# Linformer attention and an MLP mixer: the first batch's front part in head pairs with TensorE transposes, its up-projections all ahead, and another order of loads

## The chip, the cores and the metric

The kernel runs on one core of a Trainium2 chip. The metric is the device time of one execution in microseconds (us); smaller is better. Before the change the median of three runs is 519.97 us (519.9 to 520.43).

## The reference

Eight batches, 8 heads, 1024 positions, 64 dimensions a head, all inputs float32:

```python
k_proj = np.einsum('ks,bhsd->bhkd', E, k)        # 64 x 64 per head
v_proj = np.einsum('ks,bhsd->bhkd', F, v)
scores = (1.0 / np.sqrt(64)) * np.matmul(q, k_proj.transpose(0, 1, 3, 2))
attn = softmax(scores)                            # over 64 columns
x = np.matmul(attn, v_proj)                       # then heads side by side: batch x 1024 x 512
xt = x.transpose(0, 2, 1)
h = np.maximum(xt @ w_tok1, 0.0) @ w_tok2         # 1024 -> 256 -> 1024, over positions
u = x + h.transpose(0, 2, 1)
h2 = np.maximum(u @ w_ch1, 0.0) @ w_ch2           # 512 -> 1536 -> 512, over channels
out = u + h2
```

## The kernel before

Everything on the chip is bfloat16, with float32 sums in PSUM. The work of a batch has two parts.

The **front part** (`front_units`) makes `u`. `kv_proj` contracts k and v with E and F over the positions (`kv_ps`), `k_transpose` turns the projected keys (`kt_ps`, `kT`), `scores` multiplies them with the transposed queries `qT` for two heads at a time and takes the exponential (`s_ps`, `a_sb`), `attend` multiplies with the projected values for one head and divides by the sum (`o_ps` of line 195, `rdn`, `x_sb`). Then come the token mixing, `token1` (2 pieces, `h_ps`, `hT_sb`) and `token2` (8 pieces, `u_ps`, `u_sb`): each piece of `token1` needs x of all heads. Two transposes are done by DMA, issued by SyncE (SP): q into `qT`, in two halves of four heads (line 133), and `u_sb` into `uT`, in two halves of 512 positions (line 229).

The **back part** (`back_blocks`) mixes the channels in two halves of 512 positions: 12 blocks of `ch1` (4 matmuls each, the up-projection, `g_ps`, then a ReLU on ScalarE into `gT`), then 12 blocks of `ch2` (4 matmuls each, the down-projection, `o_ps` of line 265; every third one ends a row block, which VectorE adds to `u_sb` and SP sends out). That is 192 matmuls of 512 columns in a batch.

Batch 0's front part is written first, alone. After it the back part of batch b is written with the front units of batch b + 1 strewn between its blocks (lines 299 to 304). The queue of each engine is in order, but a scheduler sets that order from the written one, so the order that counts is that of the built program. All loads go through GpSimd's DMA queue (POOL) and turn float32 into bfloat16: E, F, then batch 0 (four pieces of two heads each for k, v and q), the token weights, `wc1_sb` in four pieces, `wc2_sb` in four pieces, batch 1 (two pieces each for k, v and q), batch 2 and so on. `k_sb`, `v_sb`, `q_sb` and `qT` have two buffers each. PSUM pools: `psC` three buffers (`g_ps`, `o_ps` of line 265), `psA` two (`s_ps`, `o_ps` of line 195), `psS` one (`kv_ps`, `kt_ps`, `h_ps`, `u_ps`). `out_pool` has four buffers for `o_sb`.

Of the kernel before, what the change touches and what calls it, by code (L numbers as in the profile page):

```python
# [15 lines left out]
def kernel(  # L16
# [13 lines left out]
    nc = tc.nc  # L30
# [37 lines left out]
    def load(b, parts):  # L68
        tiles = []
        for name, src in (("k_sb", k), ("v_sb", v), ("q_sb", q)):  # L70
            tiles.append(kv_pool.tile([P, H, NSI, D], BF16, tag=name, name=name))
# [32 lines left out]
    loaded[1] = load(1, 2)  # L104
# [23 lines left out]
    def front_units(b):  # L128
# [18 lines left out]
        def kv_proj():  # L147
# [86 lines left out]
        units = [kv_proj, k_transpose]  # L234
# [11 lines left out]
    def back_blocks(b):  # L246
# [4 lines left out]
        def ch1(i, cc):  # L251
# [83 lines left out]
```

## Time and profile before

| what | value |
|---|---|
| median of 3 runs | 519.97 us |
| the profiled execution's own time | 519.9 us |
| its span, first to last instruction | 517.9 us |
| outside the span | 2.0 us |
| TensorE (PE) busy | 449.0 us, 87% |
| VectorE (DVE) and ScalarE (ACT) busy | 163.0 us and 163.2 us, 31% and 32% |
| first matmul of the back part (`g_ps`) | 88.09 us after the span's start |

In the rows below, PE is TensorE's matmuls, SP is SyncE and POOL is GpSimd; "SPq" is SP's queue, which issues DMAs. `[12.41 <-DMA qT<-q_sb]` at a row's end says that the engine was idle for 12.41 us just before and that the landing of that DMA ended the wait. `x8` is the number of instructions merged in the row. Line numbers are those of the kernel before.

### The profile page before, as it was taken

How to read it: one execution, taken by the hardware profiler on the slowest of the kernel's cores; microseconds unless marked ns; L12 is line 12 of the kernel's file. 1: busy time of each engine (PE TensorE's matmuls, PEld its weight loads, DVE VectorE, ACT ScalarE, POOL GpSimd, SP SyncE). 2: the span in 40 equal slices, each digit the busy share in tenths (PEclk: the TensorE clock that was granted, in tenths of full speed). 3: DMA queues.
4: the chain of work that ended last, by engine and by line, in shares of the span. 5: the costliest groups of instructions: out<-in, count | busy, mean ns of one | idle time of the engine just before them, and what ended most of it. 6: DMA issues, size and time to landing. Idle time of an engine off the chain costs nothing.

```text
span 517.9 us, 5765 instructions
## 1 busy us (share of the span) xinstructions
PE 449.0 (87%) x2384; PEld 209.1 (40%) x2384; DVE 163.0 (31%) x300; ACT 163.2 (32%) x265; POOL 49.0 (9%) x72
## 2 busy tenths in 40 slices
PE   1300751999999999999999999999999999999997
PEld 0100320445444444454444443544444444544443
DVE  2100530044523332253335141624242423432102
ACT  0101100544144322623162507150534144332250
POOL 7422201121020101110020002000000000000000
PEclk9999975999999999999999999999999999999999
DMA  8999999999759823993597057903111230123112
GB/s 125 207 188 197 206 197 200 186 201 182 160 117 200 171 61 104 188 181 55 146 149 177 1 143 125 199 22 102 61 42 41 78 86 27 55 62 101 42 41 81
DMA packets 105530, 63.54 MB, mean 123 GB/s; under 512 B 68641, under 2 KB 96801, under 8 KB 105505
## 3 DMA queue, kind: packets, MB, share of 16 engines
q0 software_dynamic: 29728, 29.63, 35.5%
q1 hardware_dynamic: 75776, 33.56, 25.9%
q8 instruction: 18, 0.29, 0.2%
q14 instruction: 8, 0.06, 0.0%
HBM read 59.24 MB, written 16.78 MB: 147 GB/s over the span
## 4 chain that ended last, share of the span: by engine, by line
PE 78%; DMA 12%; SPq 4%; ACT 3%; DVE 1%; POOL 1%; issue 1%; POOLq 0%; ACTq 0%
PE o_ps L265 32%; PE g_ps L254 29%; DMA q_sb<-in_q_dram 6%; PE u_ps L222 5%; PE h_ps L213 5%; DMA wc_sb<-in_moe_w_ch_dram 4%; SPq L133 4%; PE kv_ps L151 2%; PE o_ps L195 2%; PE s_ps L183 2%; DMA k_sb<-in_k_dram 1%; ACT gT L258 1%; DMA uT_172<-u_sb 1%; DVE kp_sb L156 1%; ACT kp_sb L157 1%; PE kt_ps L168 1%
## 5 line engine op out<-in xcount | busy, mean ns | idle before, releaser
L258 ACT ACTIVATE gT<-g_ps 128x512 bf16<-128x512 f32 x192 | 113.1, 600 | 224.8 <-PE g_ps L254 224.5
L265 PE MATMUL o_ps<-wc_sb,gT 128*128 128x512 bf16 x768 | 182.3, 379 | 0.0
L254 PEld LDWEIGHTS <-wc_sb 128*128 128x128 bf16 x768 | 72.7, 98 | 99.0 <-issue 19.9
L265 PEld LDWEIGHTS <-gT 128*128 128x128 bf16 x768 | 72.6, 98 | 80.1 <-issue 2.6
L226 DVE TENSOR_TENSOR u_sb<-u_ps,x_sb 128x512 bf16<-128x512 f32 x64 | 44.2, 690 | 118.0 <-PE u_ps L222 118.0
L272 DVE TENSOR_TENSOR o_sb<-o_ps,u_sb 128x512 f32<-128x512 f32 x64 | 44.2, 691 | 78.1 <-PE o_ps L265 78.1
L188 ACT ACTIVATE a_sb<-s_ps 128x1024 bf16<-128x1024 f32 x32 | 32.0, 1031 | 50.8 <-PE s_ps L183 50.6
L203 DVE TENSOR_TENSOR x_sb<-o_ps,rdn 128x512 bf16<-128x512 f32 x64 | 44.2, 691 | 2.2
L222 PE MATMUL u_ps<-hT_sb,wt_sb 128*128 128x512 bf16 x128 | 39.9, 394 | 5.4 <-DVE u_sb L226 4.7
L202 DVE RECIPROCAL rdn<-o_ps 128x8 f32<-128x8 f32 x64 | 13.1, 204 | 74.3 <-PE o_ps L195 74.3
L213 PE MATMUL h_ps<-x_sb,wt_sb 128*128 128x512 bf16 x128 | 32.0, 395 | 1.7 <-DVE x_sb L203 1.1
L183 PE MATMUL s_ps<-qT,kT 64*64 64x512 bf16 x128 | 12.5, 423 | 24.3 <-DMA qT<-q_sb 24.1
L75 POOL DMA_DIRECT2D k_sb<-in_k_dram x18 | 13.5, 750 | 150.4 <-PE kv_ps L152 137.9
L195 PEld LDWEIGHTS <-a_sb 128*128 128x128 bf16 x256 | 20.2, 102 | 17.7 <-DVE x_sb L203 3.1
L222 PEld LDWEIGHTS <-wt_sb 128*128 128x128 bf16 x128 | 18.5, 145 | 21.2 <-issue 11.1
L151 PE MATMUL kv_ps<-k_sb,ET_sb 128*64 128x512 bf16 x64 | 17.2, 413 | 9.8 <-DMA k_sb<-in_k_dram 9.8
L156 DVE CAST kp_sb<-kv_ps 64x512 bf16<-64x512 f32 x8 | 5.5, 683 | 55.8 <-PE kv_ps L152 55.8
L80 POOL DMA_DIRECT2D q_sb<-in_q_dram x18 | 13.2, 739 | 101.7 <-DMA qT<-q_sb 91.9
L254 PE MATMUL g_ps<-uT_172,wc_sb 128*128 128x512 bf16 x48 | 12.1, 413 | 11.0 <-DMA uT_172<-u_sb 11.0
L213 PEld LDWEIGHTS <-wt_sb 128*128 128x128 bf16 x128 | 13.0, 101 | 18.4 <-issue 4.6
L217 ACT ACTIVATE hT_sb<-h_ps 128x512 bf16<-128x512 f32 x16 | 9.6, 597 | 27.5 <-PE h_ps L213 27.5
L152 PE MATMUL kv_ps<-v_sb,FT_sb 128*64 128x512 bf16 x64 | 17.0, 413 | 0.7 <-DMA v_sb<-in_v_dram 0.7
(54 smaller groups left out, 272.7 us busy)
## 6 DMA issues: line engine op xcount, KB each, us to landing
out_dram<-o_sb SPq DMA_DIRECT2D x64, 256.0 KB, 2.1
k_sb<-in_k_dram POOLq DMA_DIRECT2D x14, 512.0 KB, 9.7
v_sb<-in_v_dram POOLq DMA_DIRECT2D x14, 512.0 KB, 11.5
q_sb<-in_q_dram POOLq DMA_DIRECT2D x14, 512.0 KB, 8.7
wc_sb<-in_moe_w_ch_dram POOLq DMA_DIRECT2D x8, 384.0 KB, 19.3
k_sb<-in_k_dram POOLq DMA_DIRECT2D x4, 256.0 KB, 8.1
v_sb<-in_v_dram POOLq DMA_DIRECT2D x4, 256.0 KB, 8.6
q_sb<-in_q_dram POOLq DMA_DIRECT2D x4, 256.0 KB, 10.0
```

Source lines behind the costliest of these rows:

```text
L151: nc.tensor.matmul(kv_ps[0:KP], ET_sb[:, si, :], k_sb[:, :, si, :], start=a, stop=z)
L183: nc.tensor.matmul(s_ps[dst * KP : (dst + 1) * KP, h % 2, :], kT[rows, h, :], qT[rows, h].rearrange("p j s -> p (j s)"), start=True, stop= ...
L188: nc.scalar.activation(out=a_sb, in_=s_ps, func=ACT.Exp, scale=scale)
L195: nc.tensor.matmul(o_ps[:, j // 2, (j % 2) * 2 * D1 : (j % 2 + 1) * 2 * D1], a_sb[:, h % 2, j * P : (j + 1) * P], vb[:, h // 2, h % 2].rea ...
L203: nc.vector.tensor_tensor(out=x_sb[:, :, h * D : (h + 1) * D].rearrange("p (n c) d -> p n c d", n=2), in0=o4[:, :, :, 0:D], in1=rdn[:, :, ...
L213: nc.tensor.matmul(h_ps, wt1_sb[:, si, t * P : (t + 1) * P], x_sb[:, si, :], start=(si == 0), stop=(si == NSI - 1),)
L222: nc.tensor.matmul(u_ps, wt2_sb[:, t, si::NSI], hT_sb[:, t, :], start=(t == 0), stop=(t == TC - 1),)
L226: nc.vector.tensor_add(out=u_sb[:, si, :], in0=u_ps, in1=x_sb[:, si, :])
L254: nc.tensor.matmul(g_ps, wc1_sb[:, dc, cc * P : (cc + 1) * P], uT[i][:, :, dc, :], start=(dc == 0), stop=(dc == DMC - 1),)
L258: nc.scalar.activation(out=st["gT"][:, cc, :], in_=g_ps, func=ACT.Relu)
L265: nc.tensor.matmul(o2_ps, st["gT"][:, cc, ss * P : (ss + 1) * P], wc2_sb[:, cc, :], start=(cc == 0), stop=(cc == CC - 1),)
L272: nc.vector.tensor_add(out=o_sb, in0=o2_ps, in1=u_sb[:, si, :])
```

## The change

- The load function is split in two; batch 0's loads stay in their order, and batch 1's loads now stand ahead of `wc2_sb`.
- Batch 0's front part is written out by hand. `kv_proj` runs in four parts of two heads, each over columns of 128. q is transposed by TensorE (`q_transpose_pe`, eight 128x128 transposes for a head pair into `t_ps`, one copy by VectorE). The token mixing goes by head pair with 128 columns (`token1_pair`, `token2_pair`), and `u_sb` is transposed by TensorE (`u_transpose_pe`, four transposes and a copy by ScalarE). Only positions 0 to 511 of `u` are made before the back part begins, and one of the four pieces of the other half; the other three pieces and the transposes of the second half are put between the first five blocks of the back part.
- Batch 0's back part runs both up-projections first (24 blocks), then both down-projections. The front units of batch 1 start after block 16 and are spread over blocks 17 to 44.
- For the later batches, the DMA transposes of q are written with the first units of the front part and no longer ahead of all blocks.

```diff
--- before.py
+++ after.py
...
-    loaded = {0: load(0, 4)}
+
+    load_kv(0, HP)
+    load_q(0, HP)
...
+    load_kv(1, 2)
+    load_q(1, 2)
     wc2_sb = const.tile([P, CC, DM], BF16, name="wc2_sb")
     for c in range(0, CC, CC // 4):
         nc.gpsimd.dma_start(
             out=wc2_sb[:, c : c + CC // 4],
             in_=moe_w_ch2.rearrange("(cc p) d -> p cc d", p=P)[:, c : c + CC // 4],
         )
-    loaded[1] = load(1, 2)
...
-        for h in range(0, H, H // 2):
-            nc.sync.dma_start_transpose(
-                out=qT[:, h : h + H // 2].rearrange("p h j s -> p (h j) s"),
-                in_=q_sb[:, h : h + H // 2].rearrange("p h si d -> p (h si d)"),
-            )
...
+        def q_transpose_pe(hp):
+            t_ps = psC.tile([P, 2, NJ, P], BF16, tag="c", name="t_ps")
+            for h in range(2):
+                for j in range(NJ):
+                    nc.tensor.transpose(
+                        t_ps[:, h, j, :],
+                        q_sb[:, 2 * hp + h, 2 * j : 2 * j + 2, :].rearrange("p s d -> p (s d)"),
+                        ident,
+                    )
+            nc.vector.tensor_copy(out=qT[:, 2 * hp : 2 * hp + 2], in_=t_ps)
+
+        def kv_proj(parts=1):
             kv_ps = psS.tile([P, H, D], F32, tag="s", name="kv_ps")
-            for si in range(NSI):
-                a, z = si == 0, si == NSI - 1
-                nc.tensor.matmul(kv_ps[0:KP], ET_sb[:, si, :], k_sb[:, :, si, :], start=a, stop=z)
-                nc.tensor.matmul(
-                    kv_ps[KP : 2 * KP], FT_sb[:, si, :], v_sb[:, :, si, :], start=a, stop=z
-                )
+            hn = H // parts
+            for h in range(0, H, hn):
+                hs = slice(h, h + hn)
+                for si in range(NSI):
+                    a, z = si == 0, si == NSI - 1
+                    nc.tensor.matmul(
+                        kv_ps[0:KP, hs], ET_sb[:, si, :], k_sb[:, hs, si, :], start=a, stop=z
+                    )
+                    nc.tensor.matmul(
+                        kv_ps[KP : 2 * KP, hs], FT_sb[:, si, :], v_sb[:, hs, si, :],
+                        start=a, stop=z,
...
+        def token1_pair(hp):
+            cols = slice(hp * P, (hp + 1) * P)
+            h_ps = psC.tile([P, TC, P], F32, tag="c", name="hp_ps")
+            for t in range(TC):
+                for si in range(NSI):
+                    nc.tensor.matmul(
+                        h_ps[:, t, :], wt1_sb[:, si, t * P : (t + 1) * P], x_sb[:, si, cols],
+                        start=(si == 0), stop=(si == NSI - 1),
+                    )
+            nc.scalar.activation(out=hT_sb[:, :, cols], in_=h_ps, func=ACT.Relu)
+
+        def token2_pair(hp, i):
+            cols = slice(hp * P, (hp + 1) * P)
+            u_ps = psC.tile([P, NJ, P], F32, tag="c", name="up_ps")
+            for ss in range(NJ):
+                for t in range(TC):
+                    nc.tensor.matmul(
+                        u_ps[:, ss, :], wt2_sb[:, t, i * NJ + ss :: NSI], hT_sb[:, t, cols],
+                        start=(t == 0), stop=(t == TC - 1),
+                    )
+            rows = slice(i * NJ, (i + 1) * NJ)
+            nc.vector.tensor_add(out=u_sb[:, rows, cols], in0=u_ps, in1=x_sb[:, rows, cols])
+
+        def u_transpose_pe(hp, i):
+            t_ps = psA.tile([P, NJ, P], BF16, tag="a", name="ut_ps")
+            for ss in range(NJ):
+                nc.tensor.transpose(
+                    t_ps[:, ss, :], u_sb[:, i * NJ + ss, hp * P : (hp + 1) * P], ident
+                )
+            nc.scalar.copy(out=uT[i][:, :, hp, :], in_=t_ps)
+
+        if b == 0:
+            kv_proj(HP)
+            k_transpose()
+            q_transpose_pe(0)
+            q_transpose_pe(1)
+            scores(0)
+            q_transpose_pe(2)
+            scores(1)
+            attend(0)
+            attend(1)
+            q_transpose_pe(3)
+            scores(2)
+            attend(2)
+            attend(3)
+            scores(3)
+            attend(4)
+            attend(5)
+            token1_pair(0)
+            attend(6)
+            attend(7)
+            token1_pair(1)
+            token1_pair(2)
+            token2_pair(0, 0)
+            token2_pair(1, 0)
+            token1_pair(3)
+            token2_pair(2, 0)
+            u_transpose_pe(0, 0)
+            u_transpose_pe(1, 0)
+            token2_pair(3, 0)
+            u_transpose_pe(2, 0)
+            token2_pair(0, 1)
+            u_transpose_pe(3, 0)
+            return [
+                lambda: token2_pair(1, 1),
+                lambda: (u_transpose_pe(0, 1), token2_pair(2, 1)),
+                lambda: (u_transpose_pe(1, 1), token2_pair(3, 1)),
+                lambda: u_transpose_pe(2, 1),
+                lambda: u_transpose_pe(3, 1),
+            ]
+
+        units = [kv_proj, lambda: (k_transpose(), q_transpose())]
+        if b > 1:
+            units = [lambda: (q_transpose(), kv_proj()), k_transpose]
...
-            st["gT"] = gT_pool.tile([P, CC, S2], BF16, tag="gT", name="gT")
-
-        blocks = []
+            st["gT", i] = gT_pool.tile([P, CC, S2], BF16, tag="gT", name="gT")
+
+        up, down = [], []
         for i in range(2):
-            for cc in range(CC):
-                if cc == 0:
-                    blocks.append(lambda i=i: (half(i), ch1(i, 0)))
-                else:
-                    blocks.append(lambda i=i, cc=cc: ch1(i, cc))
-            for ss in range(NJ):
-                blocks += [lambda i=i, ss=ss, p=p: ch2(i, ss, p) for p in range(CC // 4)]
-        return blocks
-
-    for unit in front_units(0):
-        unit()
+            up.append([lambda i=i: (half(i), ch1(i, 0))])
+            up[i] += [lambda i=i, cc=cc: ch1(i, cc) for cc in range(1, CC)]
+            down.append(
+                [lambda i=i, ss=ss, p=p: ch2(i, ss, p) for ss in range(NJ) for p in range(CC // 4)]
+            )
+        if b == 0:
+            return up[0] + up[1] + down[0] + down[1]
+        return up[0] + down[0] + up[1] + down[1]
...
+    rest = front_units(0)
     for b in range(B):
         if b + 2 < B:
-            loaded[b + 2] = load(b + 2, 2)
+            load_kv(b + 2, 2)
+            load_q(b + 2, 2)
+        blocks = back_blocks(b)
+        n0, n1 = 2, len(blocks) - 5
+        if b == 0:
+            for block in blocks[:16]:
+                block()
+                if rest:
+                    rest.pop(0)()
+            blocks = blocks[16:]
+            n0, n1 = 0, len(blocks) - 4
         units = front_units(b + 1) if b + 1 < B else []
-        blocks = back_blocks(b)
-        first = 12 if b == 0 else 2
-        last = len(blocks) - 5
         done = 0
         for n, block in enumerate(blocks):
             block()
-            want = max(0, n + 1 - first) * len(units) // (last - first)
+            want = max(0, n + 1 - n0) * len(units) // (n1 - n0)
```

The order in which the built programs hold their instructions shows three places. The first is SP, the queue that issues the DMA transposes and the output, from its first instruction on. Before (`qT_166` is batch 0, `qT_364` batch 1, `qT_836` batch 2, `qT_1308` batch 3; `uT0_172` and `uT1_173` are the halves of batch 0):

```order
L133 DMA_TRANSPOSE qT_166<-q_sb_96 128x16x128 x2
L133 DMA_TRANSPOSE qT_364<-q_sb_125 128x16x128 x2
L229 DMA_TRANSPOSE uT0_172<-u_sb_170 128x16x128
L133 DMA_TRANSPOSE qT_836<-q_sb_357 128x16x128 x2
L229 DMA_TRANSPOSE uT1_173<-u_sb_170 128x16x128
L273 DMA out_0_dram<-o_sb_482 128x512
```

Now (`qT_694` is batch 1, `qT_1068` batch 2, `qT_1540` batch 3; `uT0_698` is batch 1):

```order
L151 DMA_TRANSPOSE qT_694<-q_sb_120 128x16x128 x2
L151 DMA_TRANSPOSE qT_1068<-q_sb_535 128x16x128 x2
L151 DMA_TRANSPOSE qT_1540<-q_sb_1061 128x16x128
L372 DMA out_0_dram<-o_sb_842 128x512
L151 DMA_TRANSPOSE qT_1540<-q_sb_1061 128x16x128
L372 DMA out_0_dram<-o_sb_882 128x512
L372 DMA out_0_dram<-o_sb_914 128x512
L372 DMA out_0_dram<-o_sb_958 128x512
L372 DMA out_0_dram<-o_sb_982 128x512
L255 DMA_TRANSPOSE uT0_698<-u_sb_696 128x16x128
```

Batch 0's transposes of q and u are gone from SP; the first output now stands behind five transposes, the last of them batch 3's.

The second place is VectorE at the start of batch 0, from the first copy of the projected keys to the keys' transpose. Before:

```order
L156 CAST kp_sb<-kv_ps 64x8x64
L163 CAST vb_132<-kv_ps 64x4x64 x2
L174 CAST kT<-kt_ps 128x512
L202 RECIPROCAL rdn<-o_ps 128x8
L203 TENSOR_TENSOR x_sb<-o_ps,rdn 128x8x64
```

Now:

```order
L182 CAST kp_sb<-kv_ps 64x8x64
L165 COPY qT<-t_ps 128x1024 x3
L189 CAST vb_132<-kv_ps 64x4x64
L165 COPY qT<-t_ps 128x1024
L189 CAST vb_132<-kv_ps 64x4x64
L200 CAST kT<-kt_ps 128x512
```

All four copies of q have moved ahead of `kT`; on TensorE all 32 transposes into `t_ps` stand ahead of `kt_ps` likewise.

The third place is ScalarE in batch 0's back part, where `gT` is the ReLU of one up-projection block, and `a_sb` the exponential of batch 1's scores. Now:

```order
L357 ACTIVATE gT<-g_ps 128x512 x13
L183 CAST kp_sb<-kv_ps 64x8x64
L188 CAST vb_138<-kv_ps 64x4x64
L357 ACTIVATE gT<-g_ps 128x512 x2
L188 CAST vb_138<-kv_ps 64x4x64
L357 ACTIVATE gT<-g_ps 128x512 x3
L214 ACTIVATE a_sb<-s_ps 128x1024 x3
L357 ACTIVATE gT<-g_ps 128x512
L214 ACTIVATE a_sb<-s_ps 128x1024
```

Before, the same stretch read:

```order
L258 ACTIVATE gT<-g_ps 128x512 x12
L157 CAST kp_sb<-kv_ps 64x8x64
L162 CAST vb_138<-kv_ps 64x4x64 x2
L188 ACTIVATE a_sb<-s_ps 128x1024 x4
L258 ACTIVATE gT<-g_ps 128x512 x8
```

Batch 1's scores now stand near the end of the 24 up-projection blocks and no longer behind the first 12 of them and most of a down-projection.

## Rows read from the trace of the kernel before

**Rows 1.** Chain of waits up to 92 us: start us, us, what.

```profile
62.75 7.01 SPq L133
...
69.81 11.81 SPq L133
...
81.66 6.39 DMA uT_172<-u_sb
...
88.09 1.01 PE g_ps L254 x2
```

**Rows 2.** Windows of one batch each: stretch, length, busy us (instructions), PEclk, DMA share, GB/s.

```profile
88.09:145.35 57.26, 56.93 (x299) 26.38 (x299) 20.04 (x36) 20.51 (x33) 6.15 (x9) 0.97 0.99 183
145.35:199.93 54.58, 54.37 (x298) 25.52 (x296) 19.99 (x36) 20.20 (x33) 4.45 (x6) 1.00 0.66 135
```

**Rows 3.** Timeline of batch 0's front: start, us, instruction, idle before and its end.

```profile
21.80 0.68 DVE L156 CAST kp_sb<-kv_ps 64x512 bf16<-64x512 f32 x1 [14.18 <-PE kv_ps L152]
...
25.59 0.69 DVE L174 CAST kT<-kt_ps 128x512 bf16<-128x512 f32 x1 [0.76 <-PE kt_ps L168]
...
37.96 1.07 PE L183 MATMUL s_ps<-qT,kT 64*64 64x512 bf16 x8 [12.41 <-DMA qT<-q_sb]
50.69 0.64 PE L183 MATMUL s_ps<-qT,kT 64*64 64x512 bf16 x4 [11.66 <-DMA qT<-q_sb]
59.16 0.69 DVE L203 TENSOR_TENSOR x_sb<-o_ps,rdn 128x512 bf16<-128x512 f32 x1
59.91 3.57 PE L213 MATMUL h_ps<-x_sb,wt_sb 128*128 128x512 bf16 x8 [1.05 <-DVE x_sb L203]
64.16 2.01 PE L213 MATMUL h_ps<-x_sb,wt_sb 128*128 128x512 bf16 x8 [0.69 <-ACT hT_sb L217]
```

**Rows 4.** Timeline of POOL's load issues; each waits for a landing eight loads earlier.

```profile
18.43 0.74 POOL L94 DMA_DIRECT2D wc_sb<-in_moe_w_ch_dram x1 [0.50 <-DMA v_sb<-in_v_dram]
23.56 0.77 POOL L100 DMA_DIRECT2D wc_sb<-in_moe_w_ch_dram x1 [0.53 <-DMA q_sb<-in_q_dram]
31.74 0.78 POOL L75 DMA_DIRECT2D k_sb<-in_k_dram x1 [2.03 <-DMA wc_sb<-in_moe_w_ch_dram]
39.96 0.74 POOL L75 DMA_DIRECT2D v_sb<-in_v_dram x1 [1.94 <-DMA wc_sb<-in_moe_w_ch_dram]
52.84 0.74 POOL L75 DMA_DIRECT2D k_sb<-in_k_dram x1 [1.77 <-DMA k_sb<-in_k_dram]
60.44 0.74 POOL L80 DMA_DIRECT2D q_sb<-in_q_dram x1 [1.80 <-DMA v_sb<-in_v_dram]
86.82 1.48 POOL L80 DMA_DIRECT2D q_sb<-in_q_dram x2 [25.64 <-DMA qT<-q_sb]
```

**Rows 5.** Timeline of SP's DMA issues.

```profile
20.77 60.85 SPq L133 DMA_TRANSPOSE qT<-q_sb  x4
86.03 9.21 SPq L133 DMA_TRANSPOSE qT<-q_sb  x2
```

**Rows 6.** Timeline of PE at the full clock.

```profile
102.49 0.40 PE L151 MATMUL kv_ps<-k_sb,ET_sb 128*64 128x512 bf16 x1
104.34 3.19 PE L265 MATMUL o_ps<-wc_sb,gT 128*128 128x512 bf16 x14
108.93 0.63 PE L183 MATMUL s_ps<-qT,kT 64*64 64x512 bf16 x8
111.53 0.39 PE L195 MATMUL o_ps<-vb_138,a_sb 128*128 128x130 bf16 x4
111.76 1.89 PE L265 MATMUL o_ps<-wc_sb,gT 128*128 128x512 bf16 x8
```

**Rows 7.** Groups by line and shape: count, busy us, mean ns of one, idle before.

```profile
L188 ACT ACTIVATE a_sb<-s_ps 128x1024 bf16<-128x1024 f32 x32 | 32.0, 1031 | 50.8 <-PE s_ps L183 50.6
L123 DVE COPY ET_sb<-e_ps 128x512 bf16<-128x512 bf16 x1 | 0.4, 425 | 1.8 <-PE e_ps L122 1.8
L122 PE MATMUL e_ps<-ident,E_sb 64*128 64x64 bf16 x8 | 0.7, 248 | 4.6 <-DMA E_sb<-in_E_dram 4.6
```

More of the change, by code (lines that the diff above doesn't have):

```diff
@@ L66, with load_kv @@
     nc.gpsimd.dma_start(out=F_sb, in_=F)
[L68 to L71, printed above, removed]
+    loaded = {}
+    def load_kv(b, parts):
+        k_sb, v_sb, q_sb = [
+            kv_pool.tile([P, H, NSI, D], BF16, tag=name, name=name) for name in ("k_sb", "v_sb", "q_sb")
+        ]
+        loaded[b] = (k_sb, v_sb, q_sb)
         hn = H // parts
         for h in range(0, H, hn):
-            for t, src in zip(tiles[:2], (k, v)):
+            for t, src in ((k_sb, k), (v_sb, v)):
                 nc.gpsimd.dma_start(
@@ L78, in load, with load_q @@
                 )
+    def load_q(b, parts):
+        hn = H // parts
         for h in range(0, H, hn):
             nc.gpsimd.dma_start(
-                out=tiles[2][:, h : h + hn],
+                out=loaded[b][2][:, h : h + hn],
                 in_=q[b, h : h + hn].rearrange("h (p si) d -> p h si d", p=P),
             )
-        return tiles
-    loaded = {0: load(0, 4)}
+    load_kv(0, HP)
+    load_q(0, HP)
     wt1_sb = const.tile([P, NSI, DT], BF16, name="wt1_sb")
@@ L145, in front_units, with q_transpose @@
         st = {}
-        def kv_proj():
-            kv_ps = psS.tile([P, H, D], F32, tag="s", name="kv_ps")
-            for si in range(NSI):
-                a, z = si == 0, si == NSI - 1
-                nc.tensor.matmul(kv_ps[0:KP], ET_sb[:, si, :], k_sb[:, :, si, :], start=a, stop=z)
-                nc.tensor.matmul(
-                    kv_ps[KP : 2 * KP], FT_sb[:, si, :], v_sb[:, :, si, :], start=a, stop=z
-                )
+        def q_transpose():
+            for h in range(0, H, H // 2):
+                nc.sync.dma_start_transpose(
+                    out=qT[:, h : h + H // 2].rearrange("p h j s -> p (h j) s"),
+                    in_=q_sb[:, h : h + H // 2].rearrange("p h si d -> p (h si d)"),
+                )
[10 more added lines that the diff above has]
+        def kv_proj(parts=1):
+            kv_ps = psS.tile([P, H, D], F32, tag="s", name="kv_ps")
+            hn = H // parts
+            for h in range(0, H, hn):
[9 more added lines that the diff above has]
+                    )
             kp_sb = small.tile([KP, H, 2, D], BF16, tag="kp_sb", name="kp_sb")
@@ L232, in token2 @@
                 )
-        units = [kv_proj, k_transpose]
+        def token1_pair(hp):
[8 more added lines that the diff above has]
+            nc.scalar.activation(out=hT_sb[:, :, cols], in_=h_ps, func=ACT.Relu)
@@ new lines, in u_transpose_pe @@
+        def u_transpose_pe(hp, i):
[3 more added lines that the diff above has]
+                    t_ps[:, ss, :], u_sb[:, i * NJ + ss, hp * P : (hp + 1) * P], ident
+                )
+            nc.scalar.copy(out=uT[i][:, :, hp, :], in_=t_ps)
[37 more added lines that the diff above has]
+                lambda: u_transpose_pe(3, 1),
+            ]
@@ L257, in ch1 @@
                 )
-            nc.scalar.activation(out=st["gT"][:, cc, :], in_=g_ps, func=ACT.Relu)
+            nc.scalar.activation(out=st["gT", i][:, cc, :], in_=g_ps, func=ACT.Relu)
         def ch2(i, ss, part):
@@ L265, in ch2 @@
                 nc.tensor.matmul(
-                    o2_ps, st["gT"][:, cc, ss * P : (ss + 1) * P], wc2_sb[:, cc, :],
+                    o2_ps, st["gT", i][:, cc, ss * P : (ss + 1) * P], wc2_sb[:, cc, :],
                     start=(cc == 0), stop=(cc == CC - 1),
@@ L275, in half @@
         def half(i):
[L276 to L278 removed]
+            st["gT", i] = gT_pool.tile([P, CC, S2], BF16, tag="gT", name="gT")
+        up, down = [], []
         for i in range(2):
[L280 to L290 removed]
+            up.append([lambda i=i: (half(i), ch1(i, 0))])
+            up[i] += [lambda i=i, cc=cc: ch1(i, cc) for cc in range(1, CC)]
+            down.append(
+                [lambda i=i, ss=ss, p=p: ch2(i, ss, p) for ss in range(NJ) for p in range(CC // 4)]
+            )
+        if b == 0:
+            return up[0] + up[1] + down[0] + down[1]
+        return up[0] + down[0] + up[1] + down[1]
+    rest = front_units(0)
     for b in range(B):
         if b + 2 < B:
[L293 removed]
+            load_kv(b + 2, 2)
[9 more added lines that the diff above has]
+            n0, n1 = 0, len(blocks) - 4
         units = front_units(b + 1) if b + 1 < B else []
[L295 to L297 removed]
         done = 0
```

## The prediction

> **What bounds the kernel now.** I read the page first: PE is busy for 87% of the span, and the slices that are not full lie in the first 90 us. The windows of one batch each say the same. From 145.35 us on a batch takes 54.58 us, of which PE is busy for 54.37 [rows 2]: there the kernel runs at PE's pace, and the change leaves those batches alone (on SP their q transposes stand among the same outputs as before). What can be won lies before 88.09 us, where the back part's first `g_ps` starts. The chain of waits shows what is there: transfers and SP's issues, the last of them the transpose of `u` [rows 1]. The timeline of the front shows two waits for DMA transposes of q, 12.41 and 11.66 us long, ahead of the scores at 37.96 and 50.69 us [rows 3]. SP then held four transposes from 20.77 to 81.62 us, and batch 0's `u` had to queue behind batch 1's q [rows 1, 5].
>
> **The program in two stretches.** Let T be the moment at which batch 0's back part starts to run densely (88.09 us now). At the full clock (2.4 GHz) a matmul of 512 columns costs 0.216 us: 14 in a row take 3.19 and 8 take 1.89, so six take 1.30 [rows 6]. From T to batch 1's third score group, PE has 95 up-projection matmuls (20.5), 24 `token2_pair` matmuls and 16 transposes (40 of 128 columns at 0.057, since four of 130 columns take 111.53 to 111.76 [rows 6]: 2.3), `kv_proj` (102.49 to 104.34: 1.85 [rows 6]), eight `kt_ps` (0.3) and two score groups (0.56; 0.63 busy [rows 6]): **25.5 us**. From that group on: 1 up-projection, 96 down-projections, 32 token matmuls of 512 columns (129 at 0.216: 27.9), two score groups and eight heads' `attend` (0.28 + 0.28 + 32 at 0.057: 2.4, less the 0.28 counted already: 2.1), then 145.35 to 517.9 us unchanged (372.55, [rows 2] and the span): **402.6 us**. Outside the span lie 2.0 us (519.9 less 517.9; the median of the runs, 519.97, agrees with that execution).
>
> **T, step by step.** Batch 0's loads keep their order, so v's last piece lands just before 18.43 and q's last just before 23.56 [rows 4]. `kv_proj` in quarters leaves one quarter after v's landing: 16 matmuls, two side by side, at the low clock, 1.2 GHz (a matmul of 512 columns takes 3.57/8 = 0.43 there [rows 3], so 128 columns 0.107): 0.9, ended at 19.4 where the first copy started at 21.80 before [rows 3]. That gain is not kept. By the built order the four q groups stand ahead of `kt_ps`, and their copies ahead of `kT`. The last group waits for q at 23.3; eight transposes take 0.9 (eight of 64 columns took 0.7 [rows 7]); its copy of 1024 elements 0.8 (512 took 0.425 [rows 7]); then one `vb` copy, `kt_ps` and `kT` as before, 2 us: scores start at **27.0**, against `kT` done at 26.28 before [rows 3]. What goes is the wait for the DMA transposes behind it. Before, the stretch from the third score group (50.69) to the last x (59.85) took 9.2 us [rows 3]; now the first two exponentials (2 x 1.03 [rows 7]) and a score group (0.7) come on top: x is complete at **39.0**. `token1_pair` for the first pairs fills PE's gaps meanwhile. After the last x PE has 16 + 24 matmuls of 128 columns and 16 transposes less those already done, about 56 x 0.057 = 3.2 us at the full clock and 6.0 at the low one, and at the end one add (0.7) and one ScalarE copy (0.6) that nothing covers, with some hand-overs: 43.5 to 46.5. If the low clock lasts from 31 us on, `token1_pair` spills over too: 49. The row for the clock: before, matmuls of 512 columns ran at 0.43 from 59.91, and after this dense run the second eight came at 2.01/8 [rows 3]. PE is dense from about 31 now, so I take the full clock for the tail: **T = 45**. The weights are no limit: the token weights follow q by about 5 us, `wc1_sb` by 13.
>
> At one place the Trainium skill speaks against this. The low-clock and full-clock prices of small matmuls above come from rows 3 and 6. By its page "TensorE: Matmul & The Clock Gate", section "Back-to-back issue gap", a stream of loads and matmuls of 128 columns sustains about 81 ns each; the trace has 57, and by 81 ns T would be 1.3 us later.
>
> **What the wait turns into.** Batch 1's q now has to be transposed by DMA while the loads still run, as batch 0's had. After q of batch 0 (23.3) the loads are the two token weights, four k and v and the first half of q of batch 1, seven of 0.5 MB at 2.53 (52.84 to 60.44 has three landings [rows 4]): 17.7; and four pieces of `wc1_sb`, between 1.9 (by bytes) and 2.74 (31.74 to 39.96, three landings, beside a transpose [rows 4]); 2.1 taken: 8.4. So SP can issue the first transpose at **49.4** (48.6 to 52). Both halves then took 29.9 us the first time (20.77 to 50.69) and 24 the second (62.75 to POOL's release at 86.82) [rows 1, 3, 4, 5]; the second is nearer, with k and v loads beside it: 73.4, rounded up for the first to **74** (72.6 to 82). The first half took 17.2 (20.77 to 37.96): 66.6, in time for the first scores at 69.3. The third score group is ready at T + 25.5 = 70.5 and waits **3.5 us** for the second half. PE, in order, stands still meanwhile.
>
> Sum: 74 + 402.6 + 2.0 = 478.6, with about 1.4 for the slow start after the wait and small stalls (57.26 against 54.58 in that batch before [rows 2]): **480 us**.
>
> What costs nothing: `wc2_sb` behind batch 1's loads lands by 60 to 63 (four pieces at 1.9 to 2.74), and the down-projections begin at T + 27 = 72. The four q copies on VectorE and eight `uT` copies on ScalarE lie beside PE in the front, as counted. The longer wait of the outputs is a rival below.
>
> **Rivals.**
> - *The transposes land in time.* For it: 24 us includes a late second half. Then T alone decides: 45 + 25.5 + 402.6 + 2 = 475, and 473.5 with T at 43.5.
> - *The front stays slow.* If TensorE's transposes run apart, not back to back, or the small matmuls don't raise the clock, T is 50 to 57: 25.5 + 402.6 + 2 + T = 480 to 487. For it: the heads' work between 50.69 and 59.85 did not raise the clock, since the matmuls from 59.91 still took 0.43 [rows 3]. Against it: eight transposes in 0.7 us [rows 7]. [...]
> - *SP's queue.* The first output now stands behind batch 3's first q transpose, whose load waits for batch 1's second half to land, and batch 2's two halves (9.21 us of issuing before [rows 5]) stand between. I reckon: q of batch 2 lands at 77 to 84 (six pieces behind `wc2_sb` at 2.5 to 3.6), its transposes are issued by 88, batch 3's first by 91, and the output has landed at 95; the fifth `o_sb` needs that buffer at about 95. If SP is 5 to 10 us later, VectorE waits, then `u_ps` and PE: 485 to 490.
> - *Slower than before.* Down-projections that wait for `wc2_sb`: it costs 1 us for each us that it lands after 72, and turns the sign only beyond 112. Four pieces would have to take 12 us each where three of `wc1_sb` took 8.2 [rows 4]. Nothing in the rows comes near it.
> - *No effect* would need another wait until 88 us for batch 0's `uT`; it has no DMA any more.
>
> **Chances.** The wait for batch 1's second half, 478 to 483: 0.50. In time: 0.23. Slow front: 0.16. SP's queue: 0.08. Slower: 0.02, no difference 0.01. I predict **480 us**. The range takes in the early end of "in time" and most of the slow front and SP's queue: **473 to 488**. About 0.2% is what a measurement of this kernel can tell from no change, and nearly all cases lie 30 us and more below: faster 0.97, same 0.01, slower 0.02.
>
> **What would show it.** In the changed kernel's profile: the first `g_ps` between 43 and 49 us; the last `t_ps` group ended by q's landing at 23 to 24; `s_ps` of batch 1 waiting for `qT` some 3 us near 70 us, with SP's first issue near 49; a span of 402 to 405 us from that group to the end. Wrong would be: `g_ps` after 50, an idle PE between 80 and 105 us ended by VectorE or by `uT`, or batches after the second that take more than 54.6 us.

## The result

The changed kernel takes **502.96 us** (median of four runs, 501.69 to 503.75), against 520.2 us (519.9 to 520.81) for the kernel before beside it: a ratio of 0.9665, with a 95% interval of 0.9642 to 0.9688. It is faster, by 17 us and not by 40: the forecast of 480 us and its range of 473 to 488 both lie below it. The profiled execution took 503.75 us, with a span of 502.0. For two experiments below (e2 and e3) all four times are given, since two of them lie 1 to 3% above the other two.

The page of the changed kernel: busy time of the engines; then, of the 40 slices of the span (12.55 us each), TensorE's busy share, its granted clock and the share of the DMA engines; last the chain of waits by engine.

```profile
PE 455.1 (91%) x2556; PEld 221.8 (44%) x2592; DVE 165.6 (33%) x304; ACT 167.3 (33%) x275; POOL 48.9 (10%) x72
...
PE   2689945975899999999999999999999999999996
...
PEclk9999995997899999999999999999999999999999
DMA  8999999999599249855592249505020411123102
...
PE 73%; DMA 19%; ACT 3%; DVE 2%; POOL 1%; issue 1%; POOLq 0%
```

TensorE is full by the fourth slice, as forecast; but the sixth and seventh (63 to 88 us), ninth and tenth (100 to 126 us) are not, and the granted clock falls in the seventh, tenth and eleventh. The DMA engines are full from the second slice to the tenth. TensorE's timeline tells the same in rows:

```profile
22.66 1.04 PE L160 MATMUL t_ps<-ident,q_sb 128*128 128x128 bf16 x8 [0.22 <-DMA q_sb<-in_q_dram]
...
26.30 1.07 PE L209 MATMUL s_ps<-qT,kT 64*64 64x512 bf16 x8 [0.79 <-DVE kT L200]
...
35.45 0.61 PE L265 MATMUL hp_ps<-x_sb,wt_sb 128*128 128x128 bf16 x7
...
36.92 1.06 PE L265 MATMUL hp_ps<-x_sb,wt_sb 128*128 128x128 bf16 x16
...
41.97 0.38 PE L353 MATMUL g_ps<-uT_170,wc_sb 128*128 128x512 bf16 x1
...
81.17 0.64 PE L209 MATMUL s_ps<-qT,kT 64*64 64x512 bf16 x4 [12.43 <-DMA qT<-q_sb]
...
116.44 1.01 PE L248 MATMUL u_ps<-hT_sb,wt_sb 128*128 128x512 bf16 x2 [6.68 <-DVE u_sb L252]
...
127.38 5.30 PE L353 MATMUL g_ps<-uT_698,wc_sb 128*128 128x512 bf16 x16 [3.64 <-DMA uT_698<-u_sb]
```

Batch 0's front part is short now: `g_ps` starts at 41.97 us, where it started at 88.09 [rows 1], and the two waits of [rows 3] in batch 0 are gone. In their place stand three others in batch 1: 12.43 us for the transposes of its q, 6.68 us for VectorE's `u_sb`, 3.64 us for its `uT`. VectorE's rows before the second of them: `u_sb` is complete for the first `uT` at 106.87 us, and then VectorE itself waits for an output to land and free its buffer:

```profile
91.32 0.69 DVE L371 TENSOR_TENSOR o_sb<-o_ps,u_sb 128x512 f32<-128x512 f32 x1
...
106.18 0.69 DVE L252 TENSOR_TENSOR u_sb<-u_ps,x_sb 128x512 bf16<-128x512 f32 x1 [0.68 <-PE u_ps L248]
...
115.10 0.69 DVE L371 TENSOR_TENSOR o_sb<-o_ps,u_sb 128x512 f32<-128x512 f32 x1 [6.85 <-DMA out_dram<-o_sb]
```

Windows of the same trace (stretch, length, busy us of PE, PEld, DVE, ACT and POOL, granted clock, DMA share, GB/s):

```profile
68.00:81.10 13.10, 0.74 (x3) 0.13 (x3) 0.00 (x0) 1.90 (x3) 0.00 (x0) 0.69 1.19 180
81.10:100.00 18.90, 18.56 (x101) 8.98 (x104) 8.75 (x19) 3.13 (x4) 5.93 (x8) 0.85 1.14 182
100.00:115.00 15.00, 9.70 (x43) 4.79 (x43) 4.75 (x7) 0.60 (x1) 1.49 (x2) 0.97 1.20 214
115.00:129.30 14.30, 9.17 (x28) 3.59 (x29) 4.05 (x6) 0.25 (x1) 0.00 (x0) 0.74 1.23 227
...
183.90:238.50 54.60, 54.12 (x293) 25.55 (x297) 20.00 (x37) 20.08 (x33) 4.45 (x6) 1.00 0.67 135
```

A later batch still takes 54.60 us (54.58 in [rows 2]). From 68 to 129 us the reader sees idle time, a granted clock of 0.69 to 0.97, so partly at the 1.2 GHz level, and DMA engines that are always full. What they carried stands in three more views. First SP's queue, then two transposes in the chain of waits (start us, us from issue to landing), then POOL's load issues:

```profile
49.14 41.83 SPq L151 DMA_TRANSPOSE qT<-q_sb  x5
91.02 1.63 SPq L372 DMA_DIRECT2D out_dram<-o_sb  x1
92.70 9.50 SPq L151 DMA_TRANSPOSE qT<-q_sb  x1
102.24 3.02 SPq L372 DMA_DIRECT2D out_dram<-o_sb  x4
106.90 15.10 SPq L255 DMA_TRANSPOSE uT_698<-u_sb  x1
```

```profile
51.68 29.44 DMA qT<-q_sb
...
106.90 20.44 DMA uT_698<-u_sb
```

```profile
49.41 0.74 POOL L78 DMA_DIRECT2D k_sb<-in_k_dram  x1 [1.53 <-DMA q_sb<-in_q_dram]
...
56.52 0.74 POOL L86 DMA_DIRECT2D q_sb<-in_q_dram  x1 [1.67 <-DMA wc_sb<-in_moe_w_ch_dram]
81.68 1.48 POOL L86 DMA_DIRECT2D q_sb<-in_q_dram  x2 [24.42 <-DMA qT<-q_sb]
91.66 1.48 POOL L86 DMA_DIRECT2D q_sb<-in_q_dram  x2 [8.50 <-DMA qT<-q_sb]
93.46 0.75 POOL L78 DMA_DIRECT2D k_sb<-in_k_dram  x1 [0.32 <-PE o_ps L221]
```

SP issued batch 1's q at 49.14 us, as forecast, but the second half, issued at 51.68, took 29.44 us to land. Later the `uT` of batch 1 took 20.44 us. Beside them went loads that nobody needed yet: q of batch 3 at 81.68 and of batch 4 at 91.66, k and v of batch 3 from 93.46. Batch 3's front part does not begin before 183.9 us.

### The profile page after: what moved, and what is told of

The parts are those of the page before. It is cut to its first block, busy times and chain, and to the rows that moved or that the text cites. A ratio compares the mean times of both kernels' runs of the same rounds, so it can differ in the third digit from the quotient of the medians.

```text
span 502.0 us, 6139 instructions
## 1 busy us (share of the span) xinstructions
PE 455.1 (91%) x2556; PEld 221.8 (44%) x2592; DVE 165.6 (33%) x304; ACT 167.3 (33%) x275; POOL 48.9 (10%) x72
## 4 chain that ended last, share of the span: by engine, by line
PE 73%; DMA 19%; ACT 3%; DVE 2%; POOL 1%; issue 1%; POOLq 0%
PE o_ps L364 31%; PE g_ps L353 26%; DMA qT<-q_sb 6%; PE h_ps L239 5%; PE u_ps L248 4%; DMA uT_698<-u_sb 4%; DMA q_sb<-in_q_dram 4%; DMA wc_sb<-in_moe_w_ch_dram 3%; PE o_ps L221 3%; PE kv_ps L174 2%; DMA v_sb<-in_v_dram 2%; PE s_ps L209 2%; ACT gT L357 1%; DMA out_dram<-o_sb 1%; DVE kp_sb L182 1%
## 5 line engine op out<-in xcount | busy, mean ns | idle before, releaser
L353 PEld LDWEIGHTS <-wc_sb 128*128 128x128 bf16 x768 | 72.6, 98 | 91.8 <-issue 13.8
L252 DVE TENSOR_TENSOR u_sb<-u_ps,x_sb 128x512 bf16<-128x512 f32 x56 | 38.6, 690 | 87.7 <-PE u_ps L248 87.7
L248 PE MATMUL u_ps<-hT_sb,wt_sb 128*128 128x512 bf16 x112 | 34.1, 387 | 6.7 <-DVE u_sb L252 6.7
L228 DVE RECIPROCAL rdn<-o_ps 128x8 f32<-128x8 f32 x64 | 13.1, 204 | 64.8 <-PE o_ps L221 64.8
L239 PE MATMUL h_ps<-x_sb,wt_sb 128*128 128x512 bf16 x106 | 26.1, 379 | 0.3
L209 PE MATMUL s_ps<-qT,kT 64*64 64x512 bf16 x128 | 12.8, 433 | 13.4 <-DMA qT<-q_sb 12.4
L248 PEld LDWEIGHTS <-wt_sb 128*128 128x128 bf16 x112 | 16.1, 144 | 19.3 <-issue 9.5
L177 PE MATMUL kv_ps<-v_sb,FT_sb 128*64 128x512 bf16 (+1 forms) x88 | 17.4, 354 | 5.3 <-DMA v_sb<-in_v_dram 5.3
L174 PE MATMUL kv_ps<-k_sb,ET_sb 128*64 128x512 bf16 (+1 forms) x88 | 18.3, 355 | 2.0 <-DMA k_sb<-in_k_dram 2.0
L239 PEld LDWEIGHTS <-wt_sb 128*128 128x128 bf16 x112 | 10.9, 98 | 13.3 <-issue 0.2
L243 ACT ACTIVATE hT_sb<-h_ps 128x512 bf16<-128x512 f32 x14 | 8.4, 597 | 25.2 <-PE h_ps L239 25.2
```

The source lines that it names most:

```text
L174: nc.tensor.matmul(kv_ps[0:KP, hs], ET_sb[:, si, :], k_sb[:, hs, si, :], start=a, stop=z)
L209: nc.tensor.matmul(s_ps[dst * KP : (dst + 1) * KP, h % 2, :], kT[rows, h, :], qT[rows, h].rearrange("p j s -> p (j s)"), start=True, stop= ...
L239: nc.tensor.matmul(h_ps, wt1_sb[:, si, t * P : (t + 1) * P], x_sb[:, si, :], start=(si == 0), stop=(si == NSI - 1),)
L248: nc.tensor.matmul(u_ps, wt2_sb[:, t, si::NSI], hT_sb[:, t, :], start=(t == 0), stop=(t == TC - 1),)
L252: nc.vector.tensor_add(out=u_sb[:, si, :], in0=u_ps, in1=x_sb[:, si, :])
L353: nc.tensor.matmul(g_ps, wc1_sb[:, dc, cc * P : (cc + 1) * P], uT[i][:, :, dc, :], start=(dc == 0), stop=(dc == DMC - 1),)
```

## The experiments

All compute the reference in full. Each time is the median of four runs, each ratio is to the kernel before, run beside it; "the change" is the 502.96 us above.

**e1, the first wait alone.** My first theory was the forecast's sum with a longer wait. Batch 1's q is loaded ahead of its k and v, so that its transposes start earlier.

```diff
-    load_kv(1, 2)
-    load_q(1, 2)
+    load_kv(1, 2, first=True)      # load_q first, then k and v
```

> Batch 1's q is loaded ahead of its k and v; nothing else changes. Theory (the wait at 81 us is the second half of batch 1's q transpose, which takes about 30 us from the landing of q whatever comes before): SP issues the two halves near 38 and 41 us, the second lands near 70, the wait of 12.4 us ahead of batch 1's third score group shrinks to 1 to 3 us and the clock does not fall there; the outputs still stand behind batch 3's transposes, so part comes back as a longer wait for the output buffer: 488 to 494 us. Rival (the transposes end when the stream of loads ends, near 81, however early they are issued): the second half still lands at 78 to 82 and the time stays at 500 to 504.

Measured: 503.81 us, ratio 0.9698 (0.9677 to 0.9719): no gain. TensorE's timeline of e1:

```profile
69.75 0.41 PE L210 MATMUL s_ps<-qT,kT 64*64 64x512 bf16 x4 [2.16 <-DMA qT<-q_sb]
...
113.87 1.01 PE L249 MATMUL u_ps<-hT_sb,wt_sb 128*128 128x512 bf16 x2 [14.84 <-DVE u_sb L253]
...
126.43 6.22 PE L354 MATMUL g_ps<-uT,wc_sb 128*128 128x512 bf16 x16 [5.37 <-DMA uT<-u_sb]
```

The edit worked, since the first wait fell from 12.43 to 2.16 us; yet the back part of batch 1 started at 126.43 us, within 1 us of the change's 127.38. What was won at 70 was lost at 114. So the sum theory fell: something else sets the moment of about 127 us.

**e2, batch 1's q by TensorE**, as batch 0's (two q halves less on SP).

```diff
+        if b == 1:
+            units = [kv_proj, k_transpose] + [lambda hp=hp: q_transpose_pe(hp) for hp in range(HP)]
```

> Batch 1's q is transposed by TensorE too, as batch 0's; 32 more transposes and four more VectorE copies. Theory (both waits come from batch 1's DMA transposes: the first directly, the second because batch 3's load of q waits for them and the outputs wait behind batch 3's transposes on SP): no wait near 68 us, the first output issued by 84, no or a short wait for the output buffer: 476 to 484 us. Rival (the outputs are held by the load of the DMA engines itself): the first wait goes, the waits between 95 and 125 us stay or grow: 488 to 495.

Measured: 492.46 and 491.32, and 502.33 and 504.59 us. No wait near 68 us in the trace (of the 492.46), but 6.08 us at 97.86 and 8.16 us at 111.47, both for VectorE, which itself waited 6.24 and 8.33 us for an output to land and free its buffer.

**e3, the order on SP's queue.** Batch 0's outputs are issued by ScalarE, so they no longer stand behind later transposes.

```diff
-                nc.sync.dma_start(out=out_v[b, :, si, :], in_=o_sb)
+                eng = nc.scalar if b == 0 else nc.sync
+                eng.dma_start(out=out_v[b, :, si, :], in_=o_sb)
```

> Batch 0's eight outputs are issued by ScalarE and not by SP. Theory (the second pair of waits, 6.9 us for the output buffer and 3.6 us for uT, is the order on SP): the output buffer is free in time, the waits for it go, uT stands behind batch 3's transposes only: 491 to 497 us, the wait at 81 us as it was. Rival (the outputs land late because the DMA engines are full, 12 us from issue to landing in the changed kernel): the outputs are issued near 88 us but still land late, 499 to 503.

Measured: 497.24, 497.76, 504.38 and 507.50 us; without the longest the ratio is 0.9625 (0.9554 to 0.9697), an interval that holds the change's 0.9665, so no gain is shown. The trace is of the longest. In it the outputs still took 8.8 us to land (median of six), and the wait for VectorE had gone into one of 16.23 us for `uT` at 129.99. That `uT` was still on SP: its `u_sb` was complete at 105.75 us, and SP, busy with batch 3's transposes, issued it at 114.74. So e3 takes the outputs out of the order on SP, and not `uT`. The Trainium skill, page "DMA: Bandwidth & Descriptors", section "Issuing engines are not separate DMA queues", says that DMAs of every issuing engine end on the same 16 DMA engines and interleave there; this trace agrees, with those 8.8 us.

**e4, the old order of the back part** (up, down, up, down), so that batch 0's first outputs leave early.

```diff
-        if b == 0:
-            return up[0] + up[1] + down[0] + down[1]
```

> Batch 0's back part in the old order (up, down, up, down by halves), the rest as changed. Theory (running both up-projections first costs nothing by itself, but puts eight outputs behind batch 3's transposes): the wait for batch 1's q ends at 81 to 82 us again, a wait for the second weights of some 6 us stands ahead of it inside the same time, four outputs go out ahead of batch 3's transposes and the wait for the output buffer goes: 490 to 497 us. Rival (both up-projections first is what gains, because the second weights come late): 505 to 512.

Measured: 497.93 us, ratio 0.9593 (0.9551 to 0.9635), 5 us faster than the change. Four outputs left ahead, and no wait for them remained; instead there were 1.73 and 1.72 us for `wc2_sb` near 60, 5.36 for `qT` at 80.44 and 10.25 for `uT` at 123.54. SP issued that `uT` at 107.07 us, 1.8 us after its `u_sb` was complete, and it took 16.4 us to land.

**e5, the old order of loads** (`wc2_sb` ahead of batch 1's k, v and q).

```diff
-    load_kv(1, 2)
-    load_q(1, 2)
     wc2_sb = const.tile([P, CC, DM], BF16, name="wc2_sb")
...
+    load_kv(1, 2)
+    load_q(1, 2)
```

> Only the order of loads is undone: the second weights ahead of batch 1. Batch 1's q then lands some 7 us later. Theory now (up to about 127 us the sum of all transfers that stand ahead of batch 1's uT sets the time, whatever waits for them first): the wait ahead of batch 1's third score group grows to 18 to 21 us, the later waits shrink by as much, and the time stays at 501 to 506 us. Rival (each wait adds by itself): 508 to 513.

Measured: 496.78 us, ratio 0.9548 (0.9526 to 0.9569): 6 us faster than the change, outside what either theory had. The chain of waits in e5:

```profile
58.14 21.01 DMA qT<-q_sb
```

Issued 6.5 us later than in the change (58.14 against 51.68), that half landed 2 us earlier (79.15 against 81.12). In the change four loads of batch 2 were issued after SP's first transpose (49.41 to 56.52 above); in e5 the last load was issued at 53.34, before SP's first transpose at 55.60.

**The second theory.** Up to 127 us the DMA engines are full, so a transfer that somebody waits for lands the later the more loads go beside it; e1 moved this delay from one wait to the next, and e2 to e5 took away a part of it at most. POOL fetches each batch as soon as its buffers come free, two or three batches ahead. If that is right, holding back loads must remove the waits, although no transfer is saved. The rival: the waits belong to the queue order on SP and to the transposes themselves, and remain.

**e6, batch 3 and later held.** GpSimd copies one element (of each partition) of batch 1's `uT` into each piece that the next loads will overwrite, so that these wait for its landing (for later batches likewise, one batch on).

```diff
-    def load_kv(b, parts):
+    def load_kv(b, parts, gate=None):
...
+        if gate is not None:
+            for t in loaded[b]:
+                for h in range(0, H, H // parts):
+                    nc.gpsimd.tensor_copy(out=t[:, h, 0, 0:1], in_=gate)
...
-            load_kv(b + 2, 2)
+            load_kv(b + 2, 2, uTs[b][0][:, 0, 0, 0:1] if b else None)
```

> The loads of batch 3 and later are held until the batch two before has the first half of its uT (one element of it is copied into each piece's target by GpSimd, so that the load has to wait). Theory (loads for batch 3 and 4, not needed before 160 us, take the DMA engines from batch 1's outputs and uT): the wait ahead of the third score group stays at 12 to 13 us, those near 108 and 124 us go, uT of batch 1 lands by 105: 486 to 491 us. Rival (it is the transposes' own length): the waits stay, 498 to 504.

Measured: 488.04 us (487.68 to 488.28), ratio 0.938 (0.9364 to 0.9396). The first wait stays (12.61 us at 80.56), the two later ones are gone, as expected. The window from 81 us shows why (columns as above):

```profile
81.00:127.00 46.00, 45.41 (x247) 21.42 (x248) 19.80 (x36) 12.59 (x21) 5.17 (x12) 0.96 0.60 122
```

A DMA share of 0.60, where the change has 1.14 to 1.23, and TensorE busy for 45.41 of 46 us. The hold moves two things at once, however. With batch 3's q, its two transposes on SP come later too: they now stand behind batch 0's outputs and batch 1's `uT`, where in the change they stood ahead of `uT` and of all outputs but the first. SP's queue in e6:

```profile
87.44 16.49 SPq L376 DMA_DIRECT2D out_dram<-o_sb  x5
105.57 1.61 SPq L259 DMA_TRANSPOSE uT<-u_sb  x1
...
129.66 7.00 SPq L155 DMA_TRANSPOSE qT<-q_sb  x2
```

So e6 shows that the later waits come from what is fetched ahead for batch 3 and later, loads and transposes together. It does not split the two, and so does not rule out the order on SP as a part of it.

**e7, batch 2 alone held**, until batch 1's `qT` has landed.

```diff
...
-        if b + 2 < B:
+        if 0 < b and b + 2 < B:
             load_kv(b + 2, 2)
...
+        if b == 0:
+            units.insert(2, lambda: (load_kv(2, 2, qTs[1][:, H - 1, NJ - 1, 0:1]), load_q(2, 2)))
```

> Only the loads of batch 2 are held, until batch 1's q transpose has landed; batch 3's are not. Theory (sum of transfers): the second half lands by 60 to 68, the first wait is gone, and the same us come back as waits for the output buffer and uT near 110 to 130: 498 to 505 us. Rival (each wait adds by itself): 488 to 492.

Measured: 506.75 us, ratio 0.9752 (0.9724 to 0.978), 4 us slower than the change. `qT` landed at 62.7 us and the first wait is gone, with the transposes, outputs and `uT` in the change's order on SP; later 10.59, 8.98 and 5.19 us were waited. As in e1, the loads pushed back met the outputs and `uT`.

**e8, both held.** The edits of e6 and e7 together.

> Both holds. Theory: neither wait is left, since the loads that are taken out of the way are needed 30 to 50 us later than they came: 475 to 481 us, the first forecast for no wait at all. Rival (the held loads are then late for batches 2 and 3, or the transposes alone are too slow): waits for k or q near 105 or 165 us, 485 to 500.

Measured: **474.41 us** (474.12 to 474.79), ratio 0.9119 (0.9103 to 0.9135): the fastest of all, with e10 level with it, and just under the 475 to 481 expected. The order on SP is that of e6. TensorE is busy for 95% of the span, where the change has 91%; its page, TensorE by slices:

```profile
PE   2679999999999999999999999999999999999996
```

Its timeline of TensorE has no wait at the third score group, and batch 1's back part starts 28 us earlier than in the change:

```profile
68.22 0.41 PE L215 MATMUL s_ps<-qT,kT 64*64 64x512 bf16 x4 [0.29 <-ACT a_sb L220]
...
99.36 3.62 PE L359 MATMUL g_ps<-uT,wc_sb 128*128 128x512 bf16 x16
```

The DMA views from 42 to 127 us, the change first and e8 second (packets and bytes in all; by queue, q0 being POOL's and q1 SP's: packets, MB, share of 16 engines; issues with their count, size and median us to landing):

```profile
DMA packets 27009, 16.74 MB, mean 197 GB/s; under 512 B 15016, under 2 KB 26292, under 8 KB 27004
...
q0 software_dynamic: 11652, 11.55, 83.3%
q1 hardware_dynamic: 15352, 5.13, 36.2%
...
out_dram<-o_sb SPq DMA_DIRECT2D x6, 256.0 KB, 13.1
qT<-q_sb SPq DMA_TRANSPOSE x6, 14.0
```

```profile
DMA packets 27635, 16.46 MB, mean 194 GB/s; under 512 B 17108, under 2 KB 26264, under 8 KB 27628
...
q0 software_dynamic: 9464, 9.38, 67.6%
q1 hardware_dynamic: 18164, 6.99, 40.1%
...
out_dram<-o_sb SPq DMA_DIRECT2D x12, 256.0 KB, 2.8
qT<-q_sb SPq DMA_TRANSPOSE x6, 4.9
```

The engines moved about 16.5 MB in both. In the change 2.2 MB more of it are loads, in e8 1.9 MB more are SP's transfers, twelve outputs in place of six. What counts is not how much goes, but what goes first: an output lands in 2.8 us in place of 13.1, a transpose in 4.9 in place of 14.0.

**e9, e10, e11: the parts of the change with the holds in place.** Each is e8 with one part undone: the old order of the back part (as e4), the old order of loads (as e5), and batch 0's q by DMA:

```diff
+            q_transpose()
...
-            q_transpose_pe(0)
-            q_transpose_pe(1)
...
-            q_transpose_pe(2)
...
-            q_transpose_pe(3)
```

> Both holds, and batch 0's back part in the old order (up, down, up, down). Theory (both up-projections first only covers the late second weights, which land by 61 us): three short waits for them between 55 and 61 us, 4 to 5 us in all, and nothing else: 477 to 480 us. Rival (it also keeps the later order in step): 482 or more; rival (it was worth nothing): 474 to 475.

> Both holds, and the old order of loads (second weights ahead of batch 1). Theory (with the holds the load order matters only through the landing of batch 1's q, some 7 us later, and its transposes then run beside no load at all): SP issues them near 56 us, the second half lands at 65 to 69, about when PE wants it: 474 to 477 us. Rival (the 6 us by which the old order was faster without the holds stay): 467 to 470. Rival (transposes take 23 us whatever runs beside them): 483 to 486.

> Both holds, but batch 0's q transposed by DMA again, beside the loads, the rest of the new front kept. Theory (TensorE's transposes are what moved the first back part to 42 us): the halves land near 38 and 50 us as before the change, x is complete near 59, the back part starts near 64 us: 494 to 500 us. Rival (the holds alone give the gain): 474 to 480.

e9: 478.97 us, ratio 0.9217 (0.9195 to 0.9239), 4.6 us over e8. TensorE waits for `wc2_sb`, and its granted clock, 1.00 there in e8, is 0.56 from 58.0 to 60.4 us and 0.66 from 60.4 to 67.4:

```profile
57.89 1.07 PE L370 MATMUL o_ps<-wc_sb,gT 128*128 128x512 bf16 x3 [1.77 <-DMA wc_sb<-in_moe_w_ch_dram]
60.40 5.72 PE L370 MATMUL o_ps<-wc_sb,gT 128*128 128x512 bf16 x15 [1.44 <-DMA wc_sb<-in_moe_w_ch_dram]
```

e10: 474.45 us, ratio 0.9128 (0.9113 to 0.9143), level with e8. Here batch 1's q was transposed with hardly a load beside it (POOL's queue moved 0.25 MB meanwhile), and both halves, 1 MB, were done 7.4 us after the first issue (56.28 to 63.65). Issue to landing of one half, from the view of the tile from 55 to 64 us:

```profile
DMA to landing us min/median/max: 4.7/4.9/5.2
```

e11: 495.01 us, ratio 0.9523 (0.9505 to 0.9541), 20.6 us over e8. The waits of [rows 3] are back:

```profile
37.81 1.07 PE L215 MATMUL s_ps<-qT,kT 64*64 64x512 bf16 x8 [15.27 <-DMA qT<-q_sb]
50.61 0.64 PE L215 MATMUL s_ps<-qT,kT 64*64 64x512 bf16 x4 [9.53 <-DMA qT<-q_sb]
...
62.12 0.38 PE L356 MATMUL g_ps<-uT,wc_sb 128*128 128x512 bf16 x1
```

**e12, e1's edit with e6's hold.** The edit that gave nothing in e1, once the later waits are gone.

> Batch 1's q loaded ahead of its k and v, which alone changed the time by nothing, now with the loads of batch 3 and later held. Theory (a us taken from the first wait was given back at the later ones; without those it counts in full): the first wait shrinks from 12.6 to 1 to 3 us, no other wait, 10 to 13 us less than with the hold alone: 475 to 479 us. Rival (loading q first is worth nothing): 487 to 489.

Measured: 477.35 us (476.87 to 478.78), ratio 0.918 (0.9153 to 0.9207): 10.7 us below e6. The first wait is 2.13 us, as in e1, and this time nothing takes it back.

## Why the prediction was wrong, step by step

**Right.** *The bound and T:* the later batches at 54.6 us and the first `g_ps` at 41.97 us, 3 us before the T of 45 and a us before the 43 to 49 named as its sign; scores at 26.30 (27.0), the last x done at 38.3 (39.0), the last q group at 22.66 with eight transposes in 1.04 us (0.9). *SP's first issue:* 49.14 us (49.4). *The program behind T:* the third score group was ready at 81.17 - 12.43 = 68.74 us (70.5), so that the stretch from T took 26.8 us for the 25.5 reckoned. The rival "the front stays slow" was false: the matmuls of 128 columns took 0.61 us for seven from 35.45 on and 1.06 for sixteen from 36.92, the pace of 2.4 GHz. Two figures of the Trainium skill's page "TensorE: Matmul & The Clock Gate" don't fit here. Its 81 ns ("Back-to-back issue gap") stand against 1.06/16 = 66 ns at most, and its 275 ns for a transpose ("Part 4: PE-mode transpose") against 1.04/8 = 130 ns from 22.66 us on.

**Failed, first step: the landing of batch 1's second half, taken as 74, was 81.12 us.** The text took the 24 us of the second pair of transposes before over the 29.9 us of the first, "with k and v loads beside it". They took 32.0 us (49.14 to 81.12). The 24 us came from a place where POOL had issued its last load at 60.44 [rows 4] and SP its first transpose at 62.75 [rows 1]; here four loads came after SP's first issue. With hardly a load beside them the same two transposes take 7.4 us (e10), so most of the term, 24.6 of the 32.0 us, is the price of what goes beside, which has no fixed size. With batch 2's loads held the wait is gone (e7 against the change, e8 against e6, each pair with one order on SP up to there). The wait was 12.43 us, not 3.5. This step costs 81.17 - 74 = 7.2 us. The text's own bounds for the landing, 72.6 to 82, held it, and by itself it would have left the time at 487, inside the range.

**Failed, second step: the 402.6 us from the third score group to the end, taken as free of further waits, were 420.8** (502.0 - 81.17), 18.2 us more. 46.2 us went by until 127.38, where the sum has 27.9 + 2.1 = 30.0; of these 16.2 us, 10.3 are the waits of 6.68 and 3.64 us. e8, with neither wait and a granted clock of 1.00, takes 31.1 us for the same work (68.22 to 99.36), so the sum itself was 1.1 us short. The other 4.8 lie mostly in stretches partly at the lower clock: from 81.10 to 100 us and from 115 to 129.3 us the granted clock is 0.85 and 0.74. It is this step that takes the time out of the range. Behind 127.38 another 2.0 us are lost, most of it in the first 16 `g_ps` (5.30 us, and 3.62 at the full clock). Together: 480 - 1.4 (the allowance for a slow start) + 7.2 + 18.2 - 0.25 (outside the span lie 1.75 us, not 2.0) = 503.75, the profiled execution.

**The rival "SP's queue"**, held at 0.08 and priced at 485 to 490, named the right place: VectorE waited 6.85 us for an output buffer, then `u_ps` and TensorE. Its figure for the first output was near (it landed at 98.6 us, 95 was reckoned). The second output, complete at 92.01 us, had to wait on SP behind batch 3's second transpose until 102.24, and then took 12.8 us to land, beside q of batch 4 and k and v of batch 3. So both its reason, the order of issues, and slow landing are in that wait, and no run splits them. Against the order alone stand e4, where four outputs leave ahead of batch 3's transposes and TensorE still waits 10.25 us for a `uT` that was issued 1.8 us after its input, and `uT` in the change itself: issued at 106.90, at once when `u_sb` was complete, it landed 20.44 us later. e3 leaves `uT` behind batch 3's transposes, and e6 moves these together with the loads.

**The mechanism that the text lacked.** It counted each transfer's delay in its own place and never summed the demand on the DMA engines up to the new end of the start-up. In the kernel before, batch 1's back part began at 145.35 us [rows 2]; with no wait it begins at 99.36 (e8), so what must land ahead of it has 46 us less, and what is fetched ahead for later batches takes the room. e6 shows the later half (14.9 us, loads and transposes of batch 3 together), e8 over e6 the first wait (13.6 us, by loads alone). With both gone the forecast's own sum comes out: 68.22 + 402.6 + 2.0 = 472.8 us, and 474.41 were measured, the time that the rival "in time" had.

**What each part of the change is worth.** With the holds: q by TensorE in batch 0 20.6 us (e11), both up-projections first 4.6 us (e9), the order of loads nothing (e10). Without them the last two cost 5 and 6 us (e4, e5). So in the kernel as changed these two edits hurt, and with the holds neither does.

**What stays open.** Why the old load order lands the transposes earlier although they are issued later (e5) was read from two traces but not tried by itself: the loads issued behind SP's first transpose are the candidate. How the 14.9 us of e6 divide between batch 3's loads and the place of its transposes on SP stays open as well. Of the new front only the transposes of q were undone by themselves; `kv_proj` in parts, the token mixing by pairs and the transposes of `u` by TensorE were not.

## What to carry to other kernels

When an edit shortens a stretch, add up all transfers that must land before its new end, and look at what is fetched ahead beside them; a wait removed where the DMA engines are full comes back at the next transfer (e1, e7), so a null result there does not show that the edit is worth nothing (e12). Tie prefetches that are not needed yet to a late result by a real dependence: a few one-element copies on GpSimd, busy for 11% of the span, were worth 28.6 us here (502.96 to 474.41). And price a DMA transpose by what goes beside it, not by another one of the same size.

## What the hardware showed unexpectedly

The same 1 MB of q, transposed by two DMAs, took 7.4 us with hardly a load beside it (e10), 23.6 beside loads already issued (e5, 55.60 to 79.15), and 32.0 where loads were still being issued (the change). A 256 KB output landed in 2.8 us (e8) or in 13.1 (the change), at 194 and 197 GB/s in all. SP itself is held meanwhile: one `uT` transpose kept it for 15.10 us. And a wait costs more than its length: after the idle 12.43 us the granted clock was 0.59 from 81.17 to 88.00 us, and the four `o_ps` at 84.72 us took 1.91 us, where four at 86.97 took 1.04.
